# The order of two streams on three engines: the chain's instructions or the dense layers' first

## The chip, the cores and the metric

One core of a Trainium2 chip. TensorE (PE in the profile) multiplies matrices, VectorE (DVE), ScalarE (ACT) and GpSimd (POOL) work element by element, SyncE (SP) issues the transfers. Each engine has a queue of its own that it runs in the order in which it was written; an instruction that waits holds up those behind it. The metric is device microseconds (us) from the start of the program to its end.

## What is computed

For 4 batches of 768 tokens and 384 features (8 heads of 48):

```
for t in range(S):                       # a recurrence over tokens
    S_re, S_im = ar*S_re - ai*S_im + k[t] v[t]^T,  ar*S_im + ai*S_re
    y[t] = q[t] @ S_re
u  = y + real(fft over tokens and features of y)
u  = u + relu(layernorm(u) @ w_ch1) @ w_ch2                    # first mixer
u  = u + (relu(u^T @ w_tok1) @ w_tok2)^T                       # token mixer
out = u + relu(u @ w_ch1') @ w_ch2'                            # second mixer
```

## The kernel before

Each batch takes two kinds of work. The **chain** is the recurrence and what hangs on it: `stage1` scans 17 small groups of steps (lines 405 to 423, L407, L410 and L411 three to a step; L353 to L385 prepare the decay factors), transposes them (L442), then goes through eight chunks of 96 tokens (scores L508 and L515, state L523 to L544, outputs L557 to L565). `stage2` folds the result (L781, L785, L794 on VectorE, a part on GpSimd), multiplies with cosines and sines (L816, L827), joins (L863, L864, L879) and normalises (L886 to L915). `transposed` (L705, L708, L709) hands the result to the dense work. Chains are numbered one to four here, by batch.

The **dense** work is all large matmuls. `mlp` goes through four quarters; in each, six groups of nine matmuls L725 fill one of three accumulators tagged `l`, ScalarE writes the high part of each (L729), VectorE the low part (L731), which also frees the accumulator; then six groups of nine matmuls L741 are added to `u` by VectorE (L744). The token mixer has L948, L954, L955 on one side and L966, L968 on the other, and ends in a `transposed` of its own. The weights of the first batch are converted on the way in `convert` (L181 to L202), a third stream called BACK.

Chain one runs alone. Then chain b+1 is written beside the dense work of batch b, up to chain four, beside which there is only the first mixer of batch three; after it everything is dense. Batches one and two have 936 dense matmuls each; the first mixer of the third has 432.

The order on each engine isn't the order of the code. Every instruction gets a priority when it is written, from the table `RANK` (rank times 100,000 plus a running number, the lower first), and a list scheduler, which goes by its own estimate of when operands are ready, takes for each engine the ready instruction of the lowest number. `RANK` has a row for TensorE ("pe"), one for the three elementwise engines ("v"), one for SyncE ("sp"), and in each a rank for CHAIN, DENSE, BACK and FIRST (chain one):

Of the kernel before, what the change touches and what calls it, by code (L numbers as in the profile page):

```python
# [51 lines left out]
def attn_fft_mixer_kernel(ctx: ExitStack, tc: tile.TileContext, aL, xL, vL, wL, qN, kN, vN, arN, aiN,  # L52
# [2 lines left out]
    CHAIN, DENSE, BACK, FIRST = 0, 1, 2, 3  # L55
    stream = [CHAIN]
    count = [0]
    RANK = {"pe": (0, 20, 20, 0), "v": (10, 0, 5, 0), "sp": (10, 0, 5, 0)}

    class Prio:  # L60

# [4 lines left out]
        def __getattr__(self, name):  # L66
            count[0] += 1
            tc.cur_priority = RANK[self.kind][stream[0]] * 100000 + count[0]
            return getattr(self.eng, name)

    ve, se, ge = Prio(nc.vector, "v"), Prio(nc.scalar, "v"), Prio(nc.gpsimd, "v")
    te, sp = Prio(nc.tensor, "pe"), Prio(nc.sync, "sp")
# [1075 lines left out]
```

## Time and profile before

| | |
|---|---|
| three timed runs | 1119.19, 1122.74, 1122.73 us (median 1122.73) |
| profiled execution | 1119.06 us, of which 1117.3 us are the span of the profile |
| busy in the span | TensorE 89%, VectorE 71%, ScalarE 46%, GpSimd 34% |
| mean granted clock of TensorE | 0.942 of full speed |

An engine's row in the profile names line, operation and tile. "Idle before" is how long the engine stood still in front of an instruction, with the instruction that ended the wait.

### The profile page before, as it was taken

The numbers are of one execution on the slowest core, as the hardware profiler recorded it, in microseconds if no ns is written. First come the engines' busy times: TensorE is split into PE (matmuls) and PEld (weight loads), VectorE is DVE, ScalarE is ACT, GpSimd is POOL, SyncE is SP. The second block draws the span as 40 slices with busy tenths as digits, with TensorE's granted clock in tenths as the row PEclk, the third lists the DMA queues.
The fourth block names the chain that finished last, engine by engine and source line by source line (L and its number), as shares of the span: only waits on it lengthen the run. The fifth ranks groups of instructions, "written<-read, shape, count | busy, mean of one in ns | idle before, by whom it ended". The sixth has DMA issues, their size and how long they took to land.

```text
span 1117.3 us, 21048 instructions
## 1 busy us (share of the span) xinstructions
PE 994.0 (89%) x7276; PEld 927.8 (83%) x7276; DVE 797.0 (71%) x2146; ACT 516.8 (46%) x1442; POOL 375.4 (34%) x531
## 2 busy tenths in 40 slices
PE   1348887999989998799999999999986999999998
PEld 0226775888878898599998899999975999999997
DVE  5996887899999858898866879996565433433332
ACT  7763435777786415677522557662224122121111
POOL 4421879475466446222324412220342001000000
PEclk9996765899999999899999999999988999999999
DMA  6116974377666756265585336655521543544532
GB/s 214 39 40 138 246 267 174 108 267 248 212 198 227 225 150 203 61 188 162 160 214 170 110 98 179 213 155 149 129 87 34 160 133 102 183 141 128 170 99 74
DMA packets 102466, 174.67 MB, mean 156 GB/s; under 512 B 11216, under 2 KB 63568, under 8 KB 101840
## 3 DMA queue, kind: packets, MB, share of 16 engines
q1 hardware_dynamic: 102352, 173.24, 51.1%
q8 instruction: 60, 0.98, 0.4%
q14 instruction: 54, 0.44, 0.1%
HBM read 133.88 MB, written 39.32 MB: 155 GB/s over the span
## 4 chain that ended last, share of the span: by engine, by line
PE 67%; DVE 14%; DMA 3%; ACT 3%; issue 2%; POOL 2%; SPq 0%; POOLq 0%; DVEq 0%; ACTq 0%
PE l L741 23%; PE l L725 22%; PE s L508 3%; PE s L816 3%; PE s L827 2%; PE s L442 2%; DMA cvt<-wL 2%; PE s L557 2%; PE s L563 1%; PE s L948 1%; DVE cvt L194 1%; DVE ws L781 1%; PE l L966 1%; PE s L966 1%; PE s L523 1%
## 5 line engine op out<-in xcount | busy, mean ns | idle before, releaser
L741 PE MATMUL l<-w,h 128*128 128x384 f32 x1728 | 331.5, 344 | 13.5 <-DVE h L731 10.0
L725 PE MATMUL l<-th,w 128*128 128x384 f32 x1152 | 314.6, 342 | 4.0 <-DVE h L731 2.0
L741 PEld LDWEIGHTS l<-w,h 128*128 128x128 f32 x1728 | 303.2, 192 | 17.2 <-DVE h L731 12.7
L725 PEld LDWEIGHTS l<-th,w 128*128 128x128 f32 x1152 | 210.6, 189 | 8.1 <-DVE h L731 4.1
L729 ACT ACTIVATE h<-l 128x384 fp32r<-128x384 f32 x192 | 94.3, 493 | 228.1 <-PE l L725 227.5
L725 PE MATMUL l<-tl,w 128*128 128x384 f32 x576 | 195.3, 339 | 0.0
L731 DVE SCALAR_TENSOR_TENSOR h<-l,h 128x384 fp32r<-128x384 f32 x192 | 106.0, 552 | 87.5 <-ACT h L729 87.1
L744 DVE TENSOR_TENSOR u<-u,l 128x384 f32<-128x384 f32 x192 | 105.3, 550 | 77.0 <-PE l L741 76.3
L442 PE MATMUL s<-misc,y 128*112 128x128 f32 x384 | 70.8, 305 | 63.9 <-DVE y L420 42.8
L442 PEld LDWEIGHTS s<-misc,y 128*112 128x112 f32 x384 | 50.2, 148 | 81.3 <-POOL A L381 18.3
L725 PEld LDWEIGHTS l<-tl,w 128*128 128x128 f32 x576 | 109.0, 189 | 0.6 <-DVE tl L709 0.3
L191 POOL TENSOR_TENSOR cvt<-cvt 128x384 int32<-128x384 int32 x56 | 62.7, 1120 | 35.4 <-DVE cvt L189 7.5
L363 POOL TENSOR_TENSOR tm<-tm 128x144 f32<-128x144 f32 (+1 forms) x68 | 36.5, 538 | 107.6 <-ACT tm L362 102.1
L508 PE MATMUL s<-qkt 112*96 112x96 f32 x512 | 60.4, 269 | 3.5 <-DVE sc L515 2.7
L407 DVE TENSOR_TENSOR p<-p,A 128x144 f32<-128x144 f32 x192 | 59.5, 310 | 2.6
L508 PEld LDWEIGHTS s<-qkt 112*96 112x96 f32 x512 | 54.4, 179 | 6.1 <-DVE sc L515 2.8
L201 POOL TENSOR_TENSOR w<-cvt,w 128x384 fp32r<-128x384 f32 x44 | 52.5, 1201 | 7.9 <-ACT w L200 4.9
L541 POOL TENSOR_TENSOR yc<-Aa,gm 48x384 f32<-48x384 f32 x18 | 21.0, 1165 | 100.8 <-DVE Aa L534 100.8
L381 POOL TENSOR_TENSOR A<-raw,tm 128x144 f32<-128x144 f32 (+1 forms) x68 | 34.3, 505 | 59.9 <-DVE yt L410 31.1
L411 DVE TENSOR_TENSOR p<-p,yt 128x96 f32<-128x96 f32 x192 | 50.1, 261 | 3.6
L933 POOL TENSOR_TENSOR xl<-u,xh 128x384 fp32r<-128x384 f32 x18 | 17.9, 1007 | 101.1 <-ACT xh L932 101.1
L353 POOL TENSOR_TENSOR tm<-sq 128x144 f32<-128x144 f32 (+1 forms) x68 | 35.2, 518 | 48.9 <-ACT sq L348 38.9
(183 smaller groups left out, 1830.8 us busy)
## 6 DMA issues: line engine op xcount, KB each, us to landing
w<-wscr SPq DMA_DIRECT2D x180, 384.0 KB, 3.5
cvt<-wL SPq DMA_DIRECT2D x56, 384.0 KB, 5.1
wscr<-w SPq DMA_DIRECT2D x44, 384.0 KB, 4.1
kn<-y SPq DMA_DIRECT2D x128, 96.0 KB, 2.2
Kn<-kn SPq DMA_DIRECT2D x64, 192.0 KB, 4.1
raw<-aL SPq DMA_DIRECT2D x52, 144.0 KB, 3.1
xx<-xL SPq DMA_DIRECT2D x52, 144.0 KB, 3.1
V<-vL SPq DMA_DIRECT2D x32, 144.0 KB, 3.3
```

Of the source, the lines that this page charges most:

```text
L191: x = ge.tensor_tensor(out=a, in0=a, in1=lo, op=ALU.add)
L201: ge.tensor_tensor(out=parts[:, 1, :], in0=a.bitcast(F32), in1=r32(parts[:, 0, :]), op=ALU.subtract)
L363: ge.tensor_tensor(out=tt, in0=x, in1=tt, op=ALU.mult)
L407: x = ve.tensor_tensor(out=cur, in0=prev, in1=A[:, j, 0:3, :], op=ALU.mult)
L411: ve.tensor_tensor(out=cur[:, 0:2, :], in0=cur[:, 0:2, :], in1=y, op=ALU.add)
L442: te.transpose(ps[:, j, :], y[:, j, 0:112], ident)
L508: te.matmul(out=ps[:, j, :], lhsT=K[:, hc, :], rhs=Q[:, hc, :])
L725: te.matmul(out=ps, lhsT=w1[:, wi, kt * 128:kt * 128 + 128], rhs=x[g][:, kt, :], start=(n == 0), stop=(n == 8))
L729: x = se.activation(out=hi, in_=ps, func=ACTF.Relu)
L731: ve.scalar_tensor_tensor(out=h[:, 1, g * 384:g * 384 + 384], in0=ps, scalar=0.0, in1=r32(hi), op0=ALU.max, op1=ALU.subtract)
L741: te.matmul(out=ps, lhsT=hs[m][:, hi, tt * 128:tt * 128 + 128], rhs=w2[:, wi, :], start=(n == 0), stop=(n == 8))
L744: ve.tensor_tensor(out=u[tt], in0=u[tt], in1=ps, op=ALU.add)
```

## The change

In the row of the elementwise engines, rank 10 moves from the chain to the dense stream. TensorE keeps the chain ahead of the dense work, SyncE keeps the dense work first. Conversions (5) stay between the two.

```
-    RANK = {"pe": (0, 20, 20, 0), "v": (10, 0, 5, 0), "sp": (10, 0, 5, 0)}
+    RANK = {"pe": (0, 20, 20, 0), "v": (0, 10, 5, 0), "sp": (10, 0, 5, 0)}
```

What the scheduler makes of it differs from before only from the first dense part on, in places like these. First, VectorE's queue after the second token product of batch one, before and then with the change, up to the third of the six L709 (`tl` is the low part of the transposed input of the second mixer, `p`, `A` and `yt` belong to the scan of chain two):

```order
L968 TENSOR_TENSOR u_1625<-u_1625,l 128x384
L383 SCALAR_TENSOR_TENSOR A<-raw,misc,tm 128x3x48
L709 TENSOR_TENSOR tl<-l,th 128x3x128
L411 TENSOR_TENSOR p<-p,yt_78 128x96
L709 TENSOR_TENSOR tl<-l,th 128x3x128
L404 TENSOR_SCALAR p<-p 128x48
L709 TENSOR_TENSOR tl<-l,th 128x3x128
```

```order
L968 TENSOR_TENSOR u_1625<-u_1625,l 128x384
L411 TENSOR_TENSOR p<-p,yt_78 128x96
L383 SCALAR_TENSOR_TENSOR A<-raw,misc,tm 128x3x48
L709 TENSOR_TENSOR tl<-l,th 128x3x128
L404 TENSOR_SCALAR p<-p 128x48
L709 TENSOR_TENSOR tl<-l,th 128x3x128
L407 TENSOR_TENSOR p<-p,A 128x144
L410 TENSOR_TENSOR yt_77<-p,A 128x96
L411 TENSOR_TENSOR p<-p,yt_77 128x96
L709 TENSOR_TENSOR tl<-l,th 128x3x128
```

Three instructions of the scan have moved from behind the third L709 to ahead of it. Second, VectorE's queue where chain three enters `stage2`, in the first quarter of batch two's second mixer, before and with the change (`ws` is the work space of `stage2`, `h` the low part of the hidden layer):

```order
L731 SCALAR_TENSOR_TENSOR h<-l,h 128x384
L781 TENSOR_TENSOR ws<-xT 112x4x288
L781 TENSOR_TENSOR ws<-xT 112x4x96
L785 TENSOR_TENSOR ws<-ws 112x2x288
L731 SCALAR_TENSOR_TENSOR h<-l,h 128x384
L785 TENSOR_TENSOR ws<-ws 112x2x288
L785 TENSOR_TENSOR ws<-ws 112x2x96 x2
L731 SCALAR_TENSOR_TENSOR h<-l,h 128x384
L785 TENSOR_TENSOR ws<-ws 112x2x288
L794 TENSOR_TENSOR ws<-ws 112x2x191 x2
L731 SCALAR_TENSOR_TENSOR h<-l,h 128x384
```

```order
L731 SCALAR_TENSOR_TENSOR h<-l,h 128x384
L781 TENSOR_TENSOR ws<-xT 112x4x288
L781 TENSOR_TENSOR ws<-xT 112x4x96
L785 TENSOR_TENSOR ws<-ws 112x2x288 x2
L731 SCALAR_TENSOR_TENSOR h<-l,h 128x384
L785 TENSOR_TENSOR ws<-ws 112x2x96 x2
L731 SCALAR_TENSOR_TENSOR h<-l,h 128x384
L785 TENSOR_TENSOR ws<-ws 112x2x288
L794 TENSOR_TENSOR ws<-ws 112x2x191 x2
L785 TENSOR_TENSOR ws<-ws 112x2x96
L744 TENSOR_TENSOR u_3328<-u_3328,l 128x384
```

Of the quarter's six L731, three are done up to the first row before and four with the change; the next stands behind one L785 before and behind two now. Third, TensorE's queue from the end of the fourth chain's chunk loop to the next transposes' neighbour L827, before and with the change (`dcos` holds the cosines):

```order
L563 MATMUL s<-qkt,T 48x96
L741 MATMUL l<-w,h 128x384 x45
L816 MATMUL s<-dcos,ws 128x97 x12
L741 MATMUL l<-w,h 128x384 x9
L816 MATMUL s<-dcos,ws 128x97 x4
L816 MATMUL s<-dcos,ws 64x97 x8
L816 MATMUL s<-dcos,ws 65x97 x4
L816 MATMUL s<-dcos,ws 63x97 x4
L827 MATMUL s<-ws 128x193 x4
```

```order
L563 MATMUL s<-qkt,T 48x96
L741 MATMUL l<-w,h 128x384 x37
L816 MATMUL s<-dcos,ws 128x97 x16
L816 MATMUL s<-dcos,ws 64x97 x8
L816 MATMUL s<-dcos,ws 65x97 x4
L816 MATMUL s<-dcos,ws 63x97 x4
L827 MATMUL s<-ws 128x193 x4
```

Of the 54 matmuls L741 that followed the chunk loop, 17 now stand ahead of its end, and none is left between the L816.

## Rows read from the trace of the kernel before

**Rows 1.** the page, part 1: busy time of each engine, share of the span, instructions
```profile
PE 994.0 (89%) x7276; PEld 927.8 (83%) x7276; DVE 797.0 (71%) x2146; ACT 516.8 (46%) x1442; POOL 375.4 (34%) x531
```

**Rows 2.** stretches: length, then busy us (instructions) of PE, PEld, DVE, ACT, POOL, clock, DMA
```profile
200.00:360.00 160.00, 147.68 (x840) 139.50 (x839) 153.12 (x427) 118.42 (x340) 93.50 (x124) 0.98 0.66 214
640.00:800.00 160.00, 160.00 (x1285) 154.19 (x1285) 126.99 (x408) 82.27 (x238) 34.20 (x66) 1.00 0.55 157
800.00:860.00 60.00, 48.16 (x377) 42.28 (x376) 37.22 (x78) 20.06 (x51) 22.31 (x22) 0.86 0.19 59
```

**Rows 3.** waits of TensorE in 200 to 440 us: total, times, longest
```profile
PE l L741 <- DVE h L731: 6.9, 4, 3.4
```

**Rows 4.** VectorE in 200 to 360 us by line: count, busy us, mean ns
```profile
L194 DVE SCALAR_TENSOR_TENSOR cvt<-cvt 128x384 int32<-128x384 int32 x29 | 20.8, 718 | 0.3
L407 DVE TENSOR_TENSOR p<-p,A 128x144 f32<-128x144 f32 x47 | 14.4, 307 | 0.3
L411 DVE TENSOR_TENSOR p<-p,yt 128x96 f32<-128x96 f32 x47 | 12.1, 257 | 0.4
L410 DVE TENSOR_TENSOR yt<-p,A 128x96 f32<-128x96 f32 x47 | 11.7, 249 | 0.4
L383 DVE SCALAR_TENSOR_TENSOR A<-raw,misc,tm 128x144 f32<-128x144 f32 x16 | 9.9, 621 | 0.0
```

**Rows 5.** the chain that ended last, in order of time: start, us, what
```profile
900.58 9.36 PE l L741 x54
```

**Rows 6.** VectorE in order of time where the third chain enters stage2: start, us, idle before
```profile
606.88 4.30 DVE L781 TENSOR_TENSOR ws<-xT 112x1152 f32<-112x1152 f32 x2 [1.65 <-PE s L563]
611.10 1.04 DVE L785 TENSOR_TENSOR ws<-ws 112x576 f32<-112x576 f32 x1
612.06 0.54 DVE L731 SCALAR_TENSOR_TENSOR h<-l,h 128x384 fp32r<-128x384 f32 x1
```

**Rows 7.** waits of TensorE in 440 to 480 us
```profile
PE s L705 <- ACT ws L913: 7.3, 3, 5.2
```

**Rows 8.** TensorE in order of time, same place as rows 6
```profile
612.66 2.54 PE L741 MATMUL l<-w,h 128*128 128x384 f32 x8 [2.07 <-DVE h L731]
616.19 3.57 PE L741 MATMUL l<-w,h 128*128 128x384 f32 x10 [0.99 <-DVE h L731]
```

**Rows 9.** TensorE in order of time at the fourth chain's end
```profile
810.56 4.95 PE L741 MATMUL l<-w,h 128*128 128x384 f32 x27
818.94 6.06 PE L741 MATMUL l<-w,h 128*128 128x384 f32 x18 [3.42 <-DVE u L744]
824.83 2.81 PE L816 MATMUL s<-dcos,ws 112*128 112x97 f32 x24
827.43 1.84 PE L741 MATMUL l<-w,h 128*128 128x384 f32 x9
829.11 4.13 PE L816 MATMUL s<-dcos,ws 112*128 112x97 f32 x40
```

**Rows 10.** VectorE in order of time, same place as rows 9
```profile
810.75 4.31 DVE L781 TENSOR_TENSOR ws<-xT 112x1152 f32<-112x1152 f32 x2 [1.65 <-PE s L563]
814.99 3.43 DVE L785 TENSOR_TENSOR ws<-ws 112x576 f32<-112x576 f32 x2
818.34 0.54 DVE L744 TENSOR_TENSOR u<-u,l 128x384 f32<-128x384 f32 x1
818.81 2.09 DVE L785 TENSOR_TENSOR ws<-ws 112x192 f32<-112x192 f32 x3
821.28 0.35 DVE L785 TENSOR_TENSOR ws<-ws 112x192 f32<-112x192 f32 x1
821.55 2.75 DVE L794 TENSOR_TENSOR ws<-ws 112x382 f32<-112x382 f32 x4
```

**Rows 11.** VectorE in 640 to 800 us by line
```profile
L383 DVE SCALAR_TENSOR_TENSOR A<-raw,misc,tm 128x144 f32<-128x144 f32 x13 | 5.4, 413 | 0.0
```

**Rows 12.** VectorE in order of time, one L194
```profile
344.27 0.54 DVE L194 SCALAR_TENSOR_TENSOR cvt<-cvt 128x384 int32<-128x384 int32 x1
```
## Prediction

> **What bounds the kernel now.** I read the page first: TensorE is busy for 89% of the span, the most of all engines [rows 1]. The change leaves TensorE's own ranks alone, so its work is the same, and only its waits can change. The table by stretch shows where they are [rows 2]. From 640 to 800 us TensorE has no gap and VectorE is 79% busy: there the order on VectorE costs nothing, because a group of nine matmuls leaves each eviction time enough. From 200 to 360 us VectorE is busy for 153.12 of 160 us, because the scan of the second chain (the chains are numbered one to four, by batch), the evictions of the first dense part and the weight conversions all want it. From 800 to 860 us TensorE loses 11.84 us: the fourth chain ends late and little dense work is left. The first 200 us hold a chain alone, and the order there is unchanged in every queue, as is that of the pure dense tail.
>
> The waits, read next, say for whom. In 200 to 440 us the dearest is L741 on VectorE's eviction L731, 6.9 us in four, the longest 3.4 us [rows 3]. The last is where the second chain enters stage2: long combinations L781 and L785 stand ahead of the eviction.
>
> **The change, term by term.** No instruction is added or removed; each engine runs its own queue in the order written. On each of the three engines the built orders differ by exchanges of neighbours: an instruction comes one to five places earlier or later, seldom more. SP keeps its ranks; its loads shift by a place or two as their producers do, and no load of dense weights falls behind a whole stage. So I count what stands ahead of the instructions for which TensorE waits. All sums are made against the profiled execution, 1119.06 us (span 1117.3 and 1.76 around it).
>
> *Term 1, VectorE's full stretch.* After the first chance of a real contest (the second token product, L955 to L709), dense evictions fall behind. The first piece of the order shows the third L709, after which the next mixer can begin: three scan instructions more stand ahead of it, L407, L410 and L411, 0.307 + 0.249 + 0.257 = 0.8 us [rows 4]. The scan gains at the dense side's cost, but by its end the same dense evictions are ahead of it in both orders, and one conversion L194 fewer, 0.7 us. On TensorE's queue the scores and the chunk loop end after 863 dense matmuls instead of 865, worth 2 x 0.173 = 0.35 us (54 matmuls take 9.36 us [rows 5]). I take +0.8 - 0.35 = **+0.45 us**. Bounds: -2.3 us if the largest overtaking, three evictions (0.54 each) and a conversion, lasts to the chain's end; +1.5 us if an eviction with five scan instructions ahead (0.3 us each) is the one waited for.
>
> *Term 2, the second chain's entry into stage2.* Before, the fifth eviction L731 of a quarter stands behind L781 twice and L785 three times, and TensorE waits 3.4 us for it. In the new order two L785 come before the fourth, which is itself what TensorE then needs to free an accumulator, and the fifth follows two short L785 later. Two L781 (4.30), two L785 (2.1) and one L731 (0.54) are 6.9 us [rows 6]; TensorE has 19 matmuls, 3.3 us, to spend before it needs the buffer: a wait of 3.6 us for 3.4. **0**; bounds -1.0 (one L785 fewer in front) and +1.0.
>
> *Term 3, the same chain's end.* TensorE waits 7.3 us for L913 before the transposes L705 [rows 7]. Dense work has run out by then in both orders. The rivals on VectorE are scan instructions of the third chain, which have the same rank in both kernels, and I count 23 of them between the first L879 and the first L709 there in both orders. **0**, bounds -1 and +1 us, three scan instructions either way.
>
> *Term 4, the third chain's entry into stage2.* Second piece of the order. Before, one L785 stands between the two L781 and the fourth eviction, and TensorE waits 2.07 and then 0.99 us [rows 8]. Now four evictions are done before L781, two L785 follow, and the fifth eviction comes after them, 4.30 + 2 x 1.04 + 0.54 = 6.9 us from the end of the chunk loop. TensorE has 11 matmuls of L725 and the first 6 of L741 that do not need it, 17 x 0.173 = 2.9 us, and waits 4.0 where it waited 3.06: **+0.9 us**. Bounds: 0 (the exchange evens out in the next groups) and +2.2 (the first L744, one place further back, is waited for too).
>
> *Term 5, the fourth chain's end.* Third piece of the order. The chunk loop now ends when 17 more dense matmuls have gone by on TensorE, because the third and so the fourth chain lag in TensorE's queue: 17 x 0.173 = 2.9 us later, since TensorE has no gap between 640 and 800 us to absorb it. What follows gets shorter, though. Before, from 810.56 to the last L816 at 833.24 are 22.7 us, in which 54 dense matmuls stand between or ahead, with a wait of 3.42 us for L744 [rows 9]. Now 37 are left, and none stands between the L816. Their start is then set by VectorE: L781 4.31, L785 3.43, 2.09 and 0.35, three L744 at 0.47 each, half of the four L794 1.38, in all 13.0 us [rows 10], with 0.6 us to get going, 13.6 us after the chunk loop. The two blocks of L816 take 2.60 and 4.06 us, so the last ends at 20.3 us, 2.4 us sooner than 22.7. Net **+0.5 us**. Bounds: +2.9 (nothing is given back) and -2.4 (the chunk loop isn't late after all).
>
> The sum is 0.45 + 0 + 0 + 0.9 + 0.5 = **+1.9 us**. The three timed runs and the profiled one stand at two values, 1119.06 and 1119.19, 1122.73 and 1122.74; the median shown, 1122.73, is 3.67 us above the profiled execution. I put the forecast on their mean, 1120.93, since either value may come up: 1122.8 us, rounded to 1122.5 because term 1's bounds reach further down than up.
>
> **The rivals.** (a) *Slower: the lag isn't repaid.* If L816 keeps its distance from the chunk loop, since L781 to L794 on VectorE decide it and not the dense matmuls, term 5 is +2.9 instead of +0.5, and the sum is +4.3 us: 1125.2. For it: VectorE works almost without a break from 810.75 to 825 us. Against it: TensorE does nine dense matmuls between two blocks of L816 today. It decides from the point where the last L816 ends over 21.8 us after the chunk loop.
>
> (b) *The chain's lead lasts.* Term 1 is then -2.3 us, and the sum -0.9: 1120.0. For it: the chain ends last at both big waits, so what it gains is time gained. Against it: the lead in the order is gone by the end of the scan.
>
> (c) *Other neighbours on GpSimd.* L383 takes 621 ns from 200 to 360 us, where GpSimd is busy for 58%, and 413 ns from 640 to 800 us, where it is busy for 21% [rows 2, 4, 11]; a single L194 that met nothing takes 0.54 us, against a mean of 718 ns [rows 4, 12]. That is 16 x 0.208 + 29 x 0.178 = 8.5 us of stretching in the fullest stretch of VectorE, and the new order lays other instructions side by side. If two thirds of it fell away, the sum would be 1.9 - 5.7 = -3.8 us: 1117.1; if it grew by a half, 1.9 + 4.3 = +6.2: 1127.1. Against both: nearly the same instructions in nearly the same order meet about as often. The Trainium skill, GPSIMD Engine Reference, section Key points, says that GpSimd shares its SBUF interfaces with VectorE and contends with VectorE instructions that have two SBUF inputs. Both named instructions have two, and the trace agrees; by that rule a new order changes durations and not places alone, and the time would leave the forecast by as much as these two sums say.
>
> (d) *The ranks decide nothing.* Then the orders would be equal; they are not, so this one is out, though most exchanges fall where TensorE doesn't wait.
>
> **How the numbers follow.** Forecast 0.47; (a) 0.25; (b) 0.12; (c) 0.08 for each side. A measurement of this kernel can tell about 0.3% from no change, 3.4 us. Faster by more: the lower side of (c) 0.08, a quarter of (b) 0.03, and 0.06 of the forecast, where several terms lie at their lower bounds, together 0.17. Slower by more: (a) but for a fifth of it, 0.20, the upper side of (c) 0.08, 0.02 of the forecast, together 0.30. The rest is 0.53. The range goes from the lower side of (c), 1116.5, to just above its upper side, 1127.5; outside lies the rest of both, about 0.15.
>
> **What the profile after would show.** TensorE without a gap from 640 to 800 us again, and the same busy time but for a few us. The waits for L731 in the first dense part a few tenths longer each. One wait of about 4 us at the third chain's entry into stage2 instead of two. Between the end of the fourth chain's chunk loop and its last L816 about 20 us instead of 22.7, with L816 in one block. The wait before L705 near 480 us at about 7 us. The forecast is wrong if that wait shrinks or grows by over 3 us, if VectorE's busy time moves by over 5 us, or if TensorE shows new waits from 640 to 800 us, where I charge nothing.

## The result: 6 us slower, and the profile after

| | before | after |
|---|---|---|
| median of five timed runs | 1122.73 us | 1129.15 us (1127.54 to 1130.00) |
| profiled execution, of it the span | 1119.06, 1117.3 | 1127.79, 1126.0 |
| ratio after to before | | 1.006, 95% interval 1.0042 to 1.0078 |

The forecast was 1122.5 us and the range ended at 1127.5: the change is slower by more than the range allowed.

The page of the kernel after, its first part, answers to [rows 1]; the table by stretch answers to [rows 2]:

```profile
PE 994.0 (88%) x7276; PEld 927.3 (82%) x7276; DVE 797.5 (71%) x2146; ACT 513.6 (46%) x1442; POOL 371.9 (33%) x531
```

```profile
200.00:360.00 160.00, 147.37 (x823) 139.75 (x824) 152.50 (x424) 116.50 (x335) 91.10 (x123) 0.96 0.64 212
640.00:800.00 160.00, 160.00 (x1211) 153.69 (x1210) 127.78 (x420) 84.34 (x246) 33.57 (x68) 1.00 0.54 157
800.00:860.00 60.00, 49.30 (x460) 43.03 (x456) 36.84 (x75) 15.89 (x44) 23.31 (x23) 0.89 0.22 68
```

Instruction counts are the same and busy times differ by 4 us at most, and from 640 to 800 us TensorE is again without a gap. So the loss has to be looked for by stage. I read five points from the timelines: the first L725, the end of the chunk loop of chains two and four (start of the first L781), the start of the last L705 of chain two, the end of the last L816 of chain four, and the end of the span. "Dense" is the number of dense matmuls that stand ahead of the fourth chunk loop's end in TensorE's queue.

| stretch, us | before | after | difference |
|---|---|---|---|
| A: first L725 to the end of chain two's chunk loop | 219.1 | 221.1 | +1.9 |
| B: from there to chain two's last L705 | 47.5 | 49.5 | +2.0 |
| C: to the end of chain four's chunk loop | 342.8 | 348.2 | +5.4 |
| D: to the last L816 of chain four | 22.5 | 22.7 | +0.2 |
| E: to the end | 284.1 | 284.4 | +0.4 |
| dense | 2250 | 2267 | +17, or 2.9 us |

The 17 matmuls (0.173 us each) are only moved from behind the chunk loop to ahead of it. Without them C is 2.5 us longer, and D and E together should be 2.9 us shorter; they are 0.6 us longer, so 3.5 us are lost there. A, B, C and the end lose 1.9 + 2.0 + 2.5 + 3.5 = 9.9 us. The spans differ by 8.7 us, because the stretch ahead of the first L725 was 1.2 us shorter in the execution of the kernel after, though its order is the same. These are single executions: over all kernels of this document that first stretch took 198.9 to 204.8 us, so a difference of a microsecond between two of them says little.

The largest piece is the fourth chain's end. TensorE in order of time in the kernel after, the place of [rows 9]:

```profile
818.68 5.13 PE L741 MATMUL l<-w,h 128*128 128x384 f32 x28
827.06 3.15 PE L741 MATMUL l<-w,h 128*128 128x384 f32 x9 [3.25 <-DVE u L744]
831.48 10.11 PE L816 MATMUL s<-dcos,ws 112*128 112x97 f32 x64 [1.27 <-ACT ws L799]
```

The order is what was foreseen: 37 dense matmuls, then the L816 in one block. Its start, 12.8 us after the chunk loop, is even 0.8 us earlier than the 13.6 foreseen. But the block takes 10.11 us, where the same 64 matmuls took 2.81 + 4.13 = 6.94 before [rows 9]. The granted clock of that stretch (start and end, length, PE busy and count, clock, DMA share, GB/s) shows why:

```profile
824.00:826.00 2.00, 0.00 (x0) 1.00 0.00 0
826.00:828.00 2.00, 0.94 (x3) 0.64 0.00 0
828.00:830.00 2.00, 2.00 (x8) 0.51 0.24 52
830.00:832.00 2.00, 0.73 (x5) 1.00 0.95 292
832.00:834.00 2.00, 2.00 (x18) 0.85 0.64 246
834.00:836.00 2.00, 2.00 (x11) 0.50 0.00 0
836.00:838.00 2.00, 2.00 (x12) 0.50 0.03 8
838.00:840.00 2.00, 2.00 (x13) 0.50 0.00 0
```

The clock falls from 1.00 to 0.50, that is from 2.4 to 1.2 GHz, twice: in the wait of 3.25 us, so that nine L741 take 3.15 us instead of 1.6, and again after the wait of 1.27 us. The L816 begin at 831.48 with the clock at 1.00, it falls under them, and most of the block runs at half. Before, the clock fell once: 18 L741 behind the wait of 3.42 us took 6.06 us instead of 3.1 [rows 9]. But those were dense matmuls that ran while the L816 waited for VectorE anyway; when the L816 came, the clock was up again. The Trainium skill, TensorE: Matmul & The Clock Gate, section HAM oscillation, describes the same for waits on transfers: the array is throttled again in the wait, and the work behind it starts at the lower rate. The trace agrees for the first wait, here one on an eviction. It does not for the second: the L816 started at the higher level, and the clock fell only under them.

The third chain's entry into stage2, the place of [rows 8] and [rows 6], TensorE and then VectorE:

```profile
616.24 1.55 PE L741 MATMUL l<-w,h 128*128 128x384 f32 x8
621.66 4.61 PE L741 MATMUL l<-w,h 128*128 128x384 f32 x16 [3.87 <-DVE h L731]
```

```profile
614.42 4.29 DVE L781 TENSOR_TENSOR ws<-xT 112x1152 f32<-112x1152 f32 x2 [1.60 <-PE s L563]
618.63 2.51 DVE L785 TENSOR_TENSOR ws<-ws 112x576 f32<-112x576 f32 x2
621.06 0.54 DVE L731 SCALAR_TENSOR_TENSOR h<-l,h 128x384 fp32r<-128x384 f32 x1
```

One wait of 3.87 us stands where two of 2.07 and 0.99 were. And in the same chain's chunk loop there is a wait that had no counterpart, for a load (TensorE in order of time):

```profile
568.65 0.23 PE L523 MATMUL s<-V,Kn 96*64 96x48 f32 x1 [1.35 <-DMA Kn<-kn]
```

The two together, 0.8 + 1.35, are 2.2 of the 2.5 us of C. At the second chain's end the waits for L705 are no longer than in [rows 7] (waits of TensorE from 440 to 480 us), and yet B is 2.0 us longer:

```profile
PE s L705 <- ACT ws L913: 6.1, 2, 4.8
PE s L705 <- DVE tl L709: 0.9, 1, 0.9
```

### The profile page after: what moved, and what is told of

Same layout as the page of the kernel before. It is cut to its first block, busy times and chain, and to the rows that moved or that the text cites. A ratio compares the mean times of both kernels' runs of the same rounds, so it can differ in the third digit from the quotient of the medians.

```text
span 1126.0 us, 21048 instructions
## 1 busy us (share of the span) xinstructions
PE 994.0 (88%) x7276; PEld 927.3 (82%) x7276; DVE 797.5 (71%) x2146; ACT 513.6 (46%) x1442; POOL 371.9 (33%) x531
## 3 DMA queue, kind: packets, MB, share of 16 engines
q1 hardware_dynamic: 102352, 173.24, 50.6%
## 4 chain that ended last, share of the span: by engine, by line
PE 68%; DVE 13%; DMA 3%; POOL 3%; issue 2%; ACT 2%; SPq 0%; POOLq 0%; DVEq 0%; ACTq 0%
PE l L741 23%; PE l L725 23%; PE s L816 3%; PE s L827 3%; PE s L508 3%; PE s L442 2%; PE s L557 2%; DMA Kn<-kn 1%; DMA cvt<-wL 1%; DVE cvt L194 1%; PE l L966 1%; PE s L563 1%; PE s L948 1%; PE s L523 1%; PE s L966 1%
## 5 line engine op out<-in xcount | busy, mean ns | idle before, releaser
L741 PE MATMUL l<-w,h 128*128 128x384 f32 x1728 | 329.6, 343 | 14.4 <-DVE h L731 11.0
L725 PE MATMUL l<-th,w 128*128 128x384 f32 x1152 | 315.8, 344 | 2.6 <-DVE h L731 1.3
L741 PEld LDWEIGHTS l<-w,h 128*128 128x128 f32 x1728 | 302.5, 191 | 18.5 <-DVE h L731 14.1
L725 PEld LDWEIGHTS l<-th,w 128*128 128x128 f32 x1152 | 212.3, 191 | 5.7 <-DVE h L731 2.3
L725 PE MATMUL l<-tl,w 128*128 128x384 f32 x576 | 196.3, 341 | 0.0
L731 DVE SCALAR_TENSOR_TENSOR h<-l,h 128x384 fp32r<-128x384 f32 x192 | 106.0, 553 | 91.0 <-ACT h L729 90.0
L744 DVE TENSOR_TENSOR u<-u,l 128x384 f32<-128x384 f32 x192 | 105.4, 549 | 75.3 <-PE l L741 74.3
L725 PEld LDWEIGHTS l<-tl,w 128*128 128x128 f32 x576 | 109.8, 191 | 0.5 <-DVE tl L709 0.3
L508 PE MATMUL s<-qkt 112*96 112x96 f32 x512 | 57.8, 261 | 10.1 <-DVE sc L515 9.3
L508 PEld LDWEIGHTS s<-qkt 112*96 112x96 f32 x512 | 51.5, 172 | 13.4 <-DVE sc L515 10.2
L410 DVE TENSOR_TENSOR yt<-p,A 128x96 f32<-128x96 f32 x192 | 48.3, 251 | 2.7
```

The lines of the kernel that those rows point to most:

```text
L410: ve.tensor_tensor(out=y, in0=prev[:, 1::-1, :], in1=A[:, j, 3:5, :], op=ALU.mult)
L508: te.matmul(out=ps[:, j, :], lhsT=K[:, hc, :], rhs=Q[:, hc, :])
L725: te.matmul(out=ps, lhsT=w1[:, wi, kt * 128:kt * 128 + 128], rhs=x[g][:, kt, :], start=(n == 0), stop=(n == 8))
L731: ve.scalar_tensor_tensor(out=h[:, 1, g * 384:g * 384 + 384], in0=ps, scalar=0.0, in1=r32(hi), op0=ALU.max, op1=ALU.subtract)
L741: te.matmul(out=ps, lhsT=hs[m][:, hi, tt * 128:tt * 128 + 128], rhs=w2[:, wi, :], start=(n == 0), stop=(n == 8))
L744: ve.tensor_tensor(out=u[tt], in0=u[tt], in1=ps, op=ALU.add)
```

## Experiments

Each kernel was timed in five rounds beside the kernel before on the same chip; the four groups below are four such sittings, in which the kernel before had medians of 1121.62, 1121.36, 1121.47 and 1121.09 us. Where an edit adds lines, the line numbers of its profile are moved by as much (L754 or L751 is then L741).

### Which engines, and which chains

e1_vector gives VectorE alone the new ranks, e3_scalar_gpsimd the other two engines alone:

```
-    RANK = {"pe": (0, 20, 20, 0), "v": (10, 0, 5, 0), "sp": (10, 0, 5, 0)}
+    RANK = {"pe": (0, 20, 20, 0), "v": (0, 10, 5, 0), "o": (10, 0, 5, 0), "sp": (10, 0, 5, 0)}
...
-    ve, se, ge = Prio(nc.vector, "v"), Prio(nc.scalar, "v"), Prio(nc.gpsimd, "v")
+    ve, se, ge = Prio(nc.vector, "v"), Prio(nc.scalar, "o"), Prio(nc.gpsimd, "o")
```

In e3 the last line reads "o", "v", "v".

> The chain goes first on VectorE alone; ScalarE and GpSimd keep the dense work first. Theory V, VectorE's order carries the loss: 5 to 7 us above before (ratio 1.005 to 1.006), as with the whole change. Rival S, ScalarE's order carries it (its evictions L729 and copies L708 come before VectorE's in each chain of evictions): at most 1.5 us above before.

> The other half: the chain goes first on ScalarE and GpSimd, VectorE keeps the dense work first. Theory V: at most 1.5 us above before. Rival S: 5 to 7 us above before. If the built order decides, whatever engine it comes from, this one too is slower by some us, since here the third chain's chunk loop ends after 1494 dense matmuls and the fourth's after 2271, later than in the changed kernel (1483 and 2267; before: 1473 and 2250).

Measured 1132.27 (ratio 1.0105, 1.0086 to 1.0123) and 1128.78 us (1.0074, 1.0052 to 1.0096). Either half alone costs what the whole costs, or more. So the loss isn't what the contests on one engine cost: theory V and rival S both fall, and the third guess of e3, that the built order decides, fits. Why e1 costs even more than the whole stays open; its profile shows the fourth chain's end as in the kernel after (37 dense matmuls, 10.11 us), but that execution, 1127.90 us, was the shortest of its five.

e4_part1 has the new ranks only while chain two and the dense work beside it are written, e7_part23 only from chain three on, e6_part3 only from chain four on; `part` counts these turns, and "o" holds the old ranks:

```
+    NEW = (1,)
...
+            kind = "o" if self.kind == "v" and part[0] not in NEW else self.kind
+            tc.cur_priority = RANK[kind][stream[0]] * 100000 + count[0]
```

In e7 it is `NEW = (2, 3)`, in e6 `NEW = (3,)`.

> The new ranks hold only for what is written in the first turn of the loop: chain two and the dense work of batch one; later parts have the old ranks. Theory A, each stage loses its own share (2.3 us up to the second chain's chunk end, 2.3 us in that chain's stage2, 2.4 us in the third chain's chunk loop, 3.1 us in the fourth chain's end): 3 to 5 us above before. Rival B, it is the lag of the third and fourth chain alone, the 17 matmuls that are not repaid: at most 1.5 us above before.

> The new ranks hold only for chains three and four and what is written beside them; the first dense part has the old order, and the third chain's chunk loop ends after 1483 dense matmuls and the fourth's after 2267, as in the changed kernel. Theory A: 3 to 5 us above before. Rival B: 6 to 7 us above before, all of the loss.

> The kernel before with the new ranks from the fourth chain on alone; the order up to the third chain's stage2 is that of before (909 and 1512 dense matmuls ahead of the second and third stage2), that of the fourth moves from 2295 to 2304. Theory P: the fourth chain's share alone, about 1 us slower than before. Theory Q: the distance to before depends on how far the order moved, and here it moved little: 0 to 2 us; not more than half of the changed kernel's loss.

Measured 1126.65 (1.0057, 1.0038 to 1.0076), 1127.74 (1.0052, 1.0035 to 1.0069) and, in the third sitting, 1121.48 us (0.9998, 0.9985 to 1.0012). So the loss isn't that of the later chains alone, but the first two parts don't add up to the whole either. From the fourth chain on the new ranks are free. Its TensorE rows at the fourth chain's end (order of time; L744 is L741, L819 L816):

```profile
822.17 5.14 PE L744 MATMUL l<-w,h 128*128 128x384 f32 x18 [3.26 <-DVE u L747]
827.15 6.81 PE L819 MATMUL s<-dcos,ws 112*128 112x97 f32 x64
```

51 dense matmuls are left there, 18 of them behind the wait, and they take the low clock upon themselves; the L816 take 6.81 us.

### Spare matmuls in TensorE's waits

f1_end_after adds 33 dense-sized matmuls into an accumulator that nobody reads to the kernel after, at the fourth chain's end; f3_end_before adds 18 to the kernel before:

```
+            def spare(n):
+                ps = palloc("p", [128, 384])
+                for _ in range(n):
+                    te.matmul(out=ps, lhsT=hs[0][:, 0, 0:128], rhs=ws.get(b, p0 + 3 * qd, 1)[:, 0, :], start=True, stop=True)
             for tt in range(6):
+                if (b, p0, qd) == (B - 2, 0, 3) and tt == END[0]:
+                    spare(END[1])
...
+            if (b, p0, qd) == (B - 2, 0, 3) and END[2]:
+                spare(END[2])
```

`END` is (5, 18, 15) in f1 and (3, 18, 0) in f3.

> The changed kernel plus 33 spare dense-sized matmuls at the fourth chain's end (between the end of its chunk loop and the first L816), written into an accumulator that nobody reads: TensorE then hardly stands still there, and nothing else is added. Theory K (the waits of TensorE cost little by themselves, but its granted clock falls in them, and the work behind them that nothing hides then runs at the lower level): the 64 L816 take about 6.7 us instead of 10.1, the last ends about 20 us after the chunk loop instead of 22.7, and the time falls by about 3 us. Theory W (VectorE and the order of its queue set the end, the clock is a companion): less than 1 us, or up to 1 us lost where a spare matmul holds up an L816.

> The kernel before plus 18 spare matmuls in its wait at the fourth chain's end (3.42 us for L744). The 18 L741 behind that wait take 6.06 us at the lower clock; with the wait filled about 3.1. Theory K says that this is hidden here, since the L816 behind them wait for VectorE until about 13.6 us after the chunk loop and started at 14.3: at most 0.7 us less. Theory W: no change.

f1_end_after took 1126.97 us (1.0058, 1.0037 to 1.0079), f3_end_before 1119.68 (0.9989, 0.9975 to 1.0002). TensorE in f1_end_after (L739 are the spare ones, L751 is L741, L828 L816):

```profile
822.12 2.24 PE L739 MATMUL p<-w,h 128*128 128x384 f32 x12
824.20 1.72 PE L751 MATMUL l<-w,h 128*128 128x384 f32 x9
825.76 1.21 PE L739 MATMUL p<-w,h 128*128 128x384 f32 x6
827.14 1.85 PE L751 MATMUL l<-w,h 128*128 128x384 f32 x9 [0.17 <-DVE u L754]
828.83 2.07 PE L739 MATMUL p<-w,h 128*128 128x384 f32 x11
831.56 3.24 PE L828 MATMUL s<-dcos,ws 112*128 112x97 f32 x24 [0.66 <-ACT ws L811]
834.58 0.95 PE L739 MATMUL p<-w,h 128*128 128x384 f32 x4
835.37 4.13 PE L828 MATMUL s<-dcos,ws 112*128 112x97 f32 x40
```

The first L816 starts no sooner than in the kernel after, 12.8 us after the chunk loop, but the 64 take 3.24 + 4.13 us, and D is 20.6 us instead of 22.7. Theory K holds at this place in the trace. The timed runs don't show the gain: the median is 2.2 us below that of the kernel after, but against the kernel before of its own sitting f1 stands at 1.0058, where the kernel after stood at 1.0060.

f2_all_after and f4_all_before are f1 and f3 with more waits filled: the second chain's entry into stage2 (18 spare matmuls) and the waits ahead of L705 at the second and fourth chain's end (40 of 97 columns, written into the transposes' own accumulator).

```
+            if i == wake:
+                for _ in range(40):
+                    te.matmul(out=px[:, 0, 0:97], lhsT=ident[0:112, :], rhs=dcos[0:112, 0, 0, 0, :], start=True, stop=True)
```

> The same with two places more: 18 spare matmuls where the second chain enters stage2 (ahead of the first L741 of that quarter, whose wait is 3.87 us in the changed kernel), and 40 spare ones of 97 columns ahead of the transposes L705 at the second and at the fourth chain's end (waits of 4.82 and 5.67 us). Theory K: at the entry the 18 L741 take about 3.2 us instead of 5.95, some 2 us of it on the path; behind the L705 waits about 2 to 3 us each are won; with the fourth chain's end in all about 10 us less than the changed kernel, so below the kernel before, without any change in the order. Theory W: no gain beyond 1 us, since the same evictions and scans are waited for.

> The kernel before with the same spare matmuls at all its places: the fourth chain's end, the second chain's entry into stage2 (19 L741 behind a wait of 3.41 us take 5.15 us), and ahead of L705 at the second and fourth chain's end (5.21 and 5.67 us). Theory K: about 1.5 us at the entry and 2 to 3 us at each of the two L705, in all 6 to 8 us less than before, a version faster than both kernels. Theory W: within 1 us of before.

Measured 1127.66 (1.0063, 1.0040 to 1.0086) and 1130.03 us (1.0081, 1.0049 to 1.0113): no gain, and for the kernel before a loss. Two things were wrong with these kernels. The 40 spare ones are 80 passes and far longer than the wait; TensorE in f4_all_before and in f2_all_after at the fourth chain's end:

```profile
853.71 9.07 PE L707 MATMUL s<-dcos,misc 112*128 112x97 f32 x80
```

```profile
852.28 17.22 PE L707 MATMUL s<-dcos,misc 112*128 112x97 f32 x80
```

9.07 us where 5.67 were to be filled, and 17.22 us where the clock had already fallen. And they moved the order: in f4 the fourth chunk loop ends after 2271 dense matmuls instead of 2250, in f2 after 2271 instead of 2267. So for L705 they tell nothing. For the second chain's entry they do: with most of the wait filled (0.80 and 0.94 us are left of 3.87) and the clock at 1.00 from 420 to 480 us, f2_all_after needs 26.0 us from chain two's chunk loop to its last L816, the kernel after 25.9. Of the 2 us that theory K expected there, these two executions show nothing.

### Is it the ranks, or the order that they happen to give

g1_scan puts only stage1 ahead of the dense work on the elementwise engines, g2_stage2 only stage2 and its transposes; g4_six_before keeps the old ranks and adds six of the 97-column matmuls at chain two's L705, where 5.2 us are idle:

```
+    PARTS, part = (0, 15), [0]
...
+            if self.kind == "v" and stream[0] == CHAIN:
+                rank = PARTS[part[0]]
```

The first of `PARTS` is stage1's rank, the second that of stage2; in g2 it is (15, 0). Dense work has 10, conversions 5, as in the kernel after. (The expectations of g4 and e6 count dense matmuls up to the first L816, the text here up to the end of the chunk loop.)

> The changed kernel, but on the three elementwise engines only the recurrence and the chunk loop (stage1) go ahead of the dense work; stage2 and its transposes go behind it again, as before. Theory P (each contest that the dense work loses costs its own share): stage2's part of the loss goes, so the second chain takes about 47.2 us from the end of its chunk loop to its last L705, as before, instead of 49.5, and the time is about 2.5 us below the changed kernel. Theory Q (almost any exchange moves the built order away from that of before, in which chains three and four end their chunk loops after fewer dense matmuls, and costs several us whatever made it): within 1.5 us of the changed kernel.

> The other half: stage2 and its transposes ahead of the dense work, stage1 behind it as before. Theory P: the second chain still takes about 49.5 us from its chunk loop to its last L705, the scan's part (0.8 us up to the end of the second scan, 2 us in the third chain) goes; about 3 us below the changed kernel. The two halves together then lose about what the changed kernel loses. Theory Q: within 1.5 us of the changed kernel, so that the halves together lose about twice as much.

> The kernel before with its own ranks, plus six spare matmuls of 97 columns (about 1.4 us) ahead of the transposes L705 at the second chain's end, where TensorE stands still for 5.2 us: a disturbance that is hidden where it stands, but moves the built order behind it, so that the third chain enters stage2 after 1539 dense matmuls instead of 1512 and the fourth after 2304 instead of 2295. Theory P: the ranks are unchanged, so within 1 us of before. Theory Q: 3 to 6 us slower than before.

Measured 1126.14 (1.0047, 1.0032 to 1.0063), 1128.50 (1.0055, 1.0036 to 1.0074) and 1127.46 us (1.0047, 1.0030 to 1.0064). g4_six_before weighs most: without any change of a rank, by a disturbance that stands in idle time, it loses about what the change loses. So a loss of this size needs no change of ranks, as theory Q has it, and the two halves together lose about 1.7 times what the whole loses, where theory P expected once and theory Q twice. g1_scan alone doesn't tell the two apart: it is 3.0 us below the kernel after by the medians and 1.5 by the ratios, where P said 2.5 and Q at most 1.5. Of theory P one piece stays: B is 47.6 us in g1_scan and 49.0 in g2_stage2. Over all kernels with at most six spare matmuls in this stretch B is 47.5 to 48.6 us where stage2 is not ahead of the dense work on VectorE (before, e3, e6, e7, f3, g1, g4, h1, h2, h3; mean 47.8) and 48.6 to 50.6 where it is (after, e1, e4, f1, g2, h4; mean 49.4).

What most of the slow orders share is seen at the fourth chain's end. TensorE in g4_six_before (L744 is L741, L819 L816):

```profile
814.54 4.43 PE L744 MATMUL l<-w,h 128*128 128x384 f32 x24
819.56 1.84 PE L744 MATMUL l<-w,h 128*128 128x384 f32 x9 [0.59 <-DVE u L747]
827.27 11.72 PE L819 MATMUL s<-dcos,ws 112*128 112x97 f32 x64 [5.87 <-ACT ws L802]
```

Only 33 dense matmuls are left, they are used up early, TensorE stands still for 5.87 us, and the block takes 11.72 us. By the number of dense matmuls left after the fourth chunk loop, the 64 L816 take: before 54, 6.94 us; e4 and e6 51, 6.81; g2 42, 8.07; after and e1 37, 10.11; e7 37, 11.46; g1, e3 and g4 33, 11.55 to 11.85. It isn't all: e4_part1 loses 5 us by the median with a short block. In its profiled execution B is 2.2 and C 3.1 us longer than before, and TensorE stands still for 5.9 us in C instead of 3.1.

### The fourth chain's wait filled in two other orders

h1_six_fill is g4_six_before, h2_scan_fill is g1_scan, each with 30 spare dense-sized matmuls written behind the last dense one (`END = (9, 0, 30)` in the edit of f1; the scheduler puts nine of them ahead of the last nine L741); h3_two_before and h4_two_after are f3 and f1 with 24 spare ones of 384 columns ahead of the third pair of the fourth chain's L705.

> g4_six_before (the old ranks, the order moved by six spare matmuls at the second chain's end) plus 30 spare dense-sized matmuls between the last dense matmul and the first L816 of the fourth chain, where TensorE stands still for 5.87 us and the 64 L816 then take 11.72 us. Theory K (the lower clock behind that wait is the loss): the block takes about 6.7 us, 5.0 us less, and the time goes from 1127.5 to about 1122.5, where the kernel before is. Rival L (the lag of the third and fourth chain is the loss, the clock only goes with it): at most 1.5 us less.

> g1_scan (recurrence and chunk loop ahead of the dense work, stage2 behind it) with the same 30 spare matmuls; there TensorE stands still for 5.85 us and the 64 L816 take 11.55 us. Theory K: 4.9 us less than g1_scan's 1126.1, about 1121.3, so not slower than the kernel before. Rival L: at most 1.5 us less.

> f3_end_before plus 24 spare matmuls of 384 columns (about 4.2 us) ahead of the third pair of the fourth chain's transposes L705, where TensorE stands still for 5.67 us. Behind it 12 L705 take 3.1 us and the first 10 L948 3.04 us at the lower clock. Theory K: these take 1.6 and 1.9 us, some 2 us less than f3_end_before: about 1117.5, faster than both kernels. Rival: L705 waits for ScalarE's L913 in any case and the L948 are the only gain, about 1 us; or the clock falls in spite of the spare matmuls and they come late, 2 to 4 us more.

> f1_end_after with the same 24 spare matmuls ahead of the third pair of the fourth chain's transposes. Theory K: about 2 us less than f1_end_after, 1125. Rival as for h3_two_before: 1 us less, or 2 to 4 us more.

h1_six_fill took 1122.30 us (1.0024, 1.0004 to 1.0045), 5.2 us less than g4_six_before, and h2_scan_fill 1122.05 (1.0027, 1.0006 to 1.0049), 4.1 less than g1_scan. Set against the kernel before, as the sittings differ, the ratio falls from 1.0047 to 1.0024 and from 1.0047 to 1.0027, which is 2.6 and 2.2 us. Both are beyond the 1.5 us of rival L, but not by more than the intervals allow. So in these two orders the low clock in one block of 64 matmuls is a large part of the loss, half of it by the ratios; the intervals leave 0.4 to 5.5 us for other causes. TensorE in h2_scan_fill (L744 spare, L756 is L741, L833 L816) and, the last line of the same place, in h1_six_fill:

```profile
819.76 1.72 PE L756 MATMUL l<-w,h 128*128 128x384 f32 x9
821.32 3.81 PE L744 MATMUL p<-w,h 128*128 128x384 f32 x21
826.71 7.23 PE L833 MATMUL s<-dcos,ws 112*128 112x97 f32 x64 [1.59 <-ACT ws L816]
```

```profile
827.86 10.42 PE L831 MATMUL s<-dcos,ws 112*128 112x97 f32 x64 [1.59 <-ACT ws L814]
```

The last line matters: with the same 1.59 us left unfilled, the clock fell in the one profiled execution (about 2 us into the block) and stayed at 1.00 in the other. That execution of h1_six_fill took 1124.47 us, that of h2_scan_fill 1120.85.

h3_two_before took 1119.82 us (0.9997, 0.9980 to 1.0014) and h4_two_after 1128.34 (1.0076, 1.0045 to 1.0107): nothing won. The L705 wait for L913 behind the spare matmuls as well, 0.18 and 2.24 us in h3, 1.54 and 2.23 in h4, and the ten L948 that follow take 3.29 and 2.94 us, about the 3.04 of before. No kernel tried is faster than the kernel before by more than can be measured.

## Why the prediction was wrong

**Term 5 is the step that failed.** It took the 17 matmuls' 2.9 us as lost ahead of the chunk loop, which is right, and 2.4 us as given back, because the last L816 would end 20.3 us after the chunk loop. It ended 22.9 us after it (818.68 to 841.59 us). The order and the start of the block were as foreseen; the length of the block was taken from [rows 9], 2.60 + 4.06 us between starts, as if it belonged to the L816, while it depends on the clock at that place: it took 10.11 us. Rival (a) named the outcome and the point that decides it, 21.8 us, but not the cause: VectorE was ready in time. f1_end_after shows the cause: with the wait filled the clock stays at 1.00 and the distance, counted the same way, is 20.8 us, which is the 20.3 of the forecast to within 0.5. None of the three signs by which the forecast was to be known as wrong appeared (the wait near 480 us is 7.0 us, VectorE's busy time moved by 0.5, no wait came from 640 to 800 us): they watched other places.

**Term 4**, +0.9 us: one wait of 3.87 us for 3.06, +0.8. Right. Not charged was the wait for the load Kn in the same chain's chunk loop, 1.35 us. It is in all orders in which the third chunk loop ends after 1483 dense matmuls (0.6 to 1.6 us in after, e1, e4, e7, f1, g2, h4) and in none of those with 1473 or 1494 (in one of them, e6, 0.6 us go to another load of the chain, V). The prediction said that no load of dense weights falls behind a stage and didn't look at the chain's own loads, which on SyncE stand behind the dense ones. That SyncE's order is the cause wasn't tried.

**Terms 2 and 3**, 0 each, were mis-sized: B is 2.0 us longer. The waits were about right, 3.87 us for 3.41 at the entry and 7.0 for 7.3 ahead of L705. But at the entry only 19 matmuls L725 run ahead of the wait now, where 17 L725 and 8 L741 ran before, so 1.0 us of dense work lies behind the wait instead of ahead of it; and 18 L741 behind it take 5.95 us where 19 took 5.15. A wait of the same length that leaves more work behind it is not the same wait. That B is longer where stage2 goes first, by 1.6 us in the mean, is shown by the two groups of kernels, though their ranges touch at 48.6 us. That the clock isn't what costs there rests on one execution of f2. Which of VectorE's exchanges it is stays open.

**Term 1**, +0.45 us, and its stretch, A: +1.9 us between the two profiled executions. In eight kernels that have the order of before up to this point (before, e6, e7, f3, f4, g4, h1, h3) A is 219.1 to 221.0 us, in seven with that of after (after, e4, f1, f2, g1, h2, h4) 218.8 to 221.1. The means are 220.0 and 220.2, so the term was right within what single executions can tell, and most of the +1.9 is their scatter. TensorE's waits didn't grow much either: it is idle for 12.6 us from 200 to 360 us, 12.3 before [rows 2].

**Rival (c)** fell. VectorE by line from 200 to 360 us, the rows that answer to [rows 4]:

```profile
L194 DVE SCALAR_TENSOR_TENSOR cvt<-cvt 128x384 int32<-128x384 int32 x29 | 21.4, 737 | 0.1
L383 DVE SCALAR_TENSOR_TENSOR A<-raw,misc,tm 128x144 f32<-128x144 f32 x16 | 9.0, 567 | 0.0
```

737 ns for 718, and 567 for 621: 0.6 us more and 0.9 us less, and VectorE's busy time is 797.5 us for 797.0. **Rival (b)** fell with A. **Rival (d)** fell in form and holds in part: the orders differ, but g4_six_before loses about as much under the old ranks. What the ranks themselves cost is seen in B alone.

The sum was made of waits and matmul counts at full clock. With the pieces as measured, 3.5 us at the fourth chain's end, 2.0 of B, 2.5 of C and 0.2 of A, it is +8.2 us. The two profiled executions differ by 8.7 us, 1127.79 - 1119.06; this is no proof of the sum, since its pieces were read from the same two. The medians differ by 6.4, because that of the kernel before lies 3.67 us above its profiled execution and that of the kernel after 1.36. Of these pieces only the first has a cause that an experiment shows; the wait for Kn in C and the growth of B are seen, and their causes stay open.

## What to carry to other kernels

A wait of TensorE has two prices: its length, and the lower clock of what runs behind it. Look which work stands behind each wait of some microseconds: filler that something else hides pays nothing, while the block that the critical chain waits for here paid up to 4.9 us on a length of 6.9. Spare matmuls in the wait won part of it back where they were shorter than the wait, though not in every execution, and the kernel before had such filler by the luck of its order. When a list scheduler makes the order, compare it with a harmless disturbance of the old order before a loss is put down to the rule that was changed.

## What the hardware showed that was not expected

The granted clock fell to half in waits of 3.25 us (after) and 5.87 us (g4), and the same 64 matmuls took 6.8 to 11.85 us by what had run ahead of them. A shorter wait can go either way: behind 1.59 us the clock stayed at 1.00 in h2 and fell to 0.50 in h1, 3.2 us for the block, with the same matmuls ahead of it. And the clock need not fall in the wait: in the kernel after and in h1 it was at 1.00 when the L816 began and fell about 2 us later. Nor do matmuls without a gap always bring it back at once: 80 passes of 97 columns took 0.113 us each in f4 and 0.215 in f2, behind the same wait of 1.09 us, in which the clock had fallen in f2 alone.
